# Moving hand-over, loads and the rows of maxima in the opening of a fused attention and MLP kernel

## The chip, the cores and the metric

The kernel runs as one program on one NeuronCore of a Trainium2 chip. The metric is the device time of one execution in microseconds (us), taken over three runs. A core has five engines that run their own instruction streams and meet only at semaphores: PE (matmul), DVE (vector), ACT (scalar and activation), POOL (general) and SP (which here only starts DMA transfers). On each engine, instructions start in the order in which they stand.

## The reference

One transformer block with adaptive layer norm: 2048 tokens, width 512, 32 heads of 16, an MLP with 1792 hidden units. All tensors are float32.

```python
mod = (_silu(c) @ w_mod).reshape(c.shape[0], 6, 1, -1)
sa, ca, ga, sb, cb, gb = (mod[:, 0], mod[:, 1], mod[:, 2], mod[:, 3], mod[:, 4], mod[:, 5])
h = _layernorm(x, axis=-1) * (1 + ca) + sa
x = x + ga * _A_ref(h, A_wqkv, A_wo)            # full attention, softmax over all 2048 keys
h = _layernorm(x, axis=-1) * (1 + cb) + sb
x = x + gb * _B_ref(h, B_w1, B_b1, B_w2)        # dense, Mish, dense
```

## The kernel before

**Stages.** The opening normalises x, transposes it to `h_h` (with a rounding remainder `h_l`) and makes the first keys and queries. Then come 512 steps (`t`), 16 for each of 32 groups of work. A group is four heads (two *pairs* of heads) by one block of 512 queries; a pair's keys stand in a tile `ka`, its queries in `qa` (five of each, used in turn). In one step PE makes the scores of one block of 128 keys for four heads (`score`, L637), ACT takes their exponential (L640), PE multiplies by the values `vg` (`pv`, L655), and beside this PE makes the scores of a *later* group once more, 128 queries by 512 keys at a time (L582), so that DVE can find the row maxima that softmax subtracts (L584). The remaining projections and the whole MLP are cut into small pieces and filled in between.

**Twenty steps ahead.** The maxima must be known before a group's scores can be exponentiated. So there is a lead of 20 steps, t = -20 to -1, in which no scores are used: PE makes products two at a time (`max_pair`, L596, 128 by 1024), DVE reduces them (L598), and PE fills the time with projections (L133), three or four slots after each pair of products. The lead has 40 such pairs of products: 32 for the first group (pairs 0 and 1), then 8 for the second group's first pair (pair 2, tiles `ka2` and `qa2`). Every second or third pair of products, ACT copies two numbers of the product to a tile `seen` (L601); later users of that bank of PSUM wait for the copy.

**The rows of maxima.** When the first group's 32 reductions are done, `neg_max` reduces once more (L611), PE transposes (L617), ACT and DVE make the tile `mt` (L619, L620), and four small DMAs write it into two rows of `qa0` and `qa1` (`put` in `max_rows`, L626). With these rows in place a score product comes out with its maximum already subtracted; the first is at t = 0.

**What sets the order.** Times are counted in half steps: `at(h, f)` (L206) runs f when the program is written at half step h, and step t covers h = 2t and 2t + 1. The lead is h = -40 to -1. What the change touches: `fin` of `qk_unit` (L253, brings the accumulator of a projection to SBUF as a high part and a remainder, and stores both), `slice_split` (L236, splits a slice of the weights the same way), the fills of `ka2`, `ka3`, `ka4` with ones (L562), `load_pair` (L332: two DMAs for `qa`, two for `ka`), `load_v` (L566), `early_prep` (L1585 on: splits the first MLP weights on POOL and stores them) and the `put` of L622.

**DMA issue.** All large transfers are issued by SP, in order. Every DMA signals one of eight completion semaphores, named DMAHW0 to DMAHW7 in the built program, which are handed out in turn to all DMAs, whatever engine issues them. Before a DMA is issued, its engine waits until the DMA that last had the same semaphore has landed.

Of the kernel before, what the change touches and what calls it, by code (L numbers as in the profile page):

```python
# [8 lines left out]
F32 = mybir.dt.float32  # L9
# [9 lines left out]
def adaln_block(ctx: ExitStack, tc: tile.TileContext, x, wqkv, wo, w1, b1, w2, c, w_mod, out):  # L19
    nc = tc.nc  # L20
# [8 lines left out]
    NB = S // TB  # L29
# [56 lines left out]
    def hi_copy(eng, hi, src):  # L86
        if eng == "a":
            nc.scalar.copy(hi, src)
        elif eng == "v":
            nc.vector.tensor_copy(hi, src)  # L90
        else:
            nc.gpsimd.tensor_scalar(hi, src, 1.0, 0.0, op0=ALU.mult, op1=ALU.add)

    def lo_sub(eng, lo, src, hi):
        (nc.gpsimd if eng == "p" else nc.vector).tensor_sub(lo, src, hi.bitcast(F32))  # L95
# [15 lines left out]
    def mm3(acc, ah, al, bh, bl, late="a"):  # L111

        n = len(ah)
        seq = ((ah, bh), (ah, bl), (al, bh)) if late == "a" else ((ah, bh), (al, bh), (ah, bl))
        seq = [(l[k], r[k]) for l, r in seq for k in range(n)]
        for i, (l, r) in enumerate(seq):
            mm(acc, l, r, i == 0, i == len(seq) - 1)
# [42 lines left out]
    def bank(tag="ms"):  # L160
        if not isinstance(tag, str):
            return tag
        return ring() if tag == "ring" else ps.tile([P, TB], F32, tag=tag, name="bk", bufs=1)
# [39 lines left out]
    def at(h, f):  # L203

        hooks.setdefault(h, []).append(f)
# [4 lines left out]
    ka = [kq.tile([P, S], F32R, name=f"ka{i}") for i in range(2)]  # L210
# [25 lines left out]
    def slice_split(kind, i, pool=None, eng="p", hi_eng="a"):  # L236
        raw = slices[kind, i]
        w = raw.shape[2]
        hi = (pool or qp).tile([P, DK, w], F32R, tag="wh", name="wh", bufs=2)
        lo = (pool or qp).tile([P, DK, w], F32R, tag="wl", name="wl", bufs=2)  # L240
        hi_copy(hi_eng, hi, raw)
        lo_sub(eng, lo, raw, hi)
        slices[kind, i] = (hi, lo)

    def qk_unit(kind, ct, tb, tag):

        wh, wl = slices[kind, ct]
        acc = bank(tag)
        ts_ = slice(tb * TB, (tb + 1) * TB)
        mm3(acc, [wh[:, k, :] for k in range(DK)], [wl[:, k, :] for k in range(DK)],  # L250
            [h_h[:, k, ts_] for k in range(DK)], [h_l[:, k, ts_] for k in range(DK)], "b")

        def fin(h=None):  # L253
            late = h is not None and -4 <= h < 3
            if late and not spares:
                for v in range(2):
                    both = ap.tile([P, DK, TB], F32R, tag=f"o_{v}", name="late", bufs=1)
                    spares.extend(both[:, i, :] for i in range(DK))
            if late:
                qh, ql = spares.pop(), spares.pop()  # L260
            else:
                qh = qp.tile([P, TB], F32R, tag="qh", name="qh", bufs=2)
                ql = qp.tile([P, TB], F32R, tag="ql", name="ql", bufs=2)
            if h is None:
                hi_copy("a", qh, acc)
                lo_sub("v", ql, acc, qh)
            else:
                qf = (ap.tile([P, TB], F32, tag=f"p{len(spares) // 2 % 2 * 2}", name="qf", bufs=3) if late else
                      pw.tile([P, TB], F32, tag="raw", name="qf", bufs=1))
                nc.scalar.copy(qf, acc)  # L270
                hi_copy("p", qh, qf)
                lo_sub("p", ql, qf, qh)
            scr, rows = (qscr, 50) if kind == 0 else (kscr, 48)

            def put():
                put_away.add((kind, ct, tb))
                o = 8 * ct * rows * S + tb * TB
                if kind == 0:
                    for r, src in enumerate((qh, qh, ql)):
                        nc.sync.dma_start(dap(scr, o + r * S, [[rows * S, 8], [3 * S, DH], [1, TB]]), src.bitcast(F32))  # L280
                    return
                hi = qh.bitcast(F32)
                twice = bass.AP(tensor=hi.tensor, offset=hi.offset, ap=[list(hi.ap)[0], [0, 2], [1, TB]])
                nc.sync.dma_start(dap(scr, o, [[3 * S, P], [2 * S, 2], [1, TB]]), twice)
                nc.sync.dma_start(dap(scr, o + S, [[3 * S, P], [1, TB]]), ql.bitcast(F32))

            put() if h is None else at(clear(h + (5 if h > 60 else 2)), put)
        return fin
# [48 lines left out]
    with ExitStack() as es:  # L337
# [65 lines left out]
        def apply_tb(tb):  # L403
            rs = rss.pop(tb)
            for i in range(4):
                xt = xts[4 * tb + i]
                nc.scalar.activation(xt, xt, AF.Identity, scale=rs[:, 1, i:i + 1], bias=rs[:, 2, i:i + 1])
# [115 lines left out]
        for tb in range(NB):  # L523
            if tb + 2 < NB:
                stats_tb(tb + 2)
            parts = []
            early = []
            for kind in (1, 0) if tb == 0 else (1,):
                fin = qk_unit(kind, 0, tb, "ring" if tb + 1 < NB else "ms")
                parts.append((pe_queue[2 * DK:], fin))  # L530
                early.append(pe_queue[:2 * DK])
                pe_queue.clear()
            if tb == 0:
                (kw, qw) = early
                early = [[m for k in range(DK) for m in (kw[k], qw[k], kw[DK + k])], qw[DK:]]
            pe_queue.extend(m for e in early for m in e)
            pe_run()
            if tb in (1, 2):
                for kc in (2 * tb - 2, 2 * tb - 1):
                    unit(v_unit(0, kc, "ring"))  # L540
            if tb + 1 < NB:
                tr_tb(tb + 1, CUT1)
            for late, fin in parts:
                pe_queue.extend(late)
                unit(fin)
            if tb + 1 < NB:
                tr_tb(tb + 1, CUT2)
            if tb + 2 < NB:
                apply_tb(tb + 2)
            if tb == 0:  # L550
                for pp in range(2):
                    load_q(pp, 48)
            for pp in range(2):
                if tb < 2:
                    load_k(pp, tb)
        slice_split(0, 1)


    kq2 = ctx.enter_context(tc.tile_pool(name="kq2", bufs=1))
    ka += [kq2.tile([P, S], F32R, name=f"ka{i}") for i in range(2, NR)]  # L560
    for t in ka[2:]:
        nc.gpsimd.memset(t.bitcast(F32), 1.0)  # L562
    ap = ctx.enter_context(tc.tile_pool(name="ap", bufs=1, reuse_waits="tile"))
    vgs = {}

    def load_v(n):  # L566
        assert {(2, n % G // 4, i) for i in range(NKC)} <= put_away
        t = ap.tile([P, VROW], F32, tag="vg", name="vg", bufs=2)
        nc.sync.dma_start(t, vscr[n % G])
        vgs[n] = t  # L570
# [44 lines left out]
    def max_rows(n, mm):  # L615
        pt = ring()
        nc.tensor.transpose(pt[:32, :P], mm.rearrange("p a v q -> p (a v q)"), ident)  # L617
        mh, mt = [ap.tile([32, P], F32R, tag=t, name=t, bufs=1) for t in ("mh", "mt")]
        nc.scalar.activation(mh, pt[:32, :P], AF.Identity, scale=-1.0)  # L619
        nc.vector.scalar_tensor_tensor(mt, mh.bitcast(F32), lows[:32], pt[:32, :P], op0=ALU.mult, op1=ALU.subtract)  # L620

        def put():  # L622
            for s in (1, 0):
                for j in range(2):
                    o = (2 * s + j) * 8
                    nc.sync.dma_start(  # L626
                        qa[(2 * n + j) % NR][64 * s + 48:64 * s + 50, :].rearrange("v (s q) -> v s q", s=4).bitcast(F32),
                        mt[o:o + 8, :].bitcast(F32))
        at(2 * (16 * n + 16 - PRO) + 2, put)
# [955 lines left out]
    def early_prep(i, h):  # L1585

        def split():
            scr, raw, hi, lo = raws[i]
            hi_copy("p", hi, raw)
            lo_sub("p", lo, raw, hi)  # L1590

        def put():
            scr, _, hi, lo = raws.pop(i)
            for v, part in enumerate((hi, lo)):
                nc.sync.dma_start(scr[:, v, :], part.bitcast(F32))

        at(h, split)
        at(h + 3, put)

    for i in range(EARLY):  # L1600
        early_prep(i, (-38, -36, -34, -32, -27, -25)[i])

    def start_preps(h, i=EARLY, turn=0, puts=()):

# [15 lines left out]
    for n in range(NIT):  # L1620
# [3 lines left out]
            at(32 * (n - 1), lambda n=n: load_pair(2 * n + 1))  # L1624
        if n > 0:
            at(32 * n - 11, lambda n=n: load_v(n))
    at(-7, lambda: load_v(0))
    at(17, lambda: load_pair(4))
    for qb in range(NB - 1):
        t0 = 32 * G * (qb + 1) + 16  # L1630
# [3 lines left out]
    at(2 * (T - 28), lambda: load_ys((0, 1)))  # L1634
    at(2 * (T - 12), lambda: load_ys((2,)))
    at(2 * T - 30, tail_loads)
    for pp, h in ((2, -22), (3, -10)):
        at(h, lambda pp=pp: load_pair(pp))
    def run_hooks(h):
        for f in hooks.pop(h, []):  # L1640
# [6 lines left out]
    t = T + 2  # L1647
# [32 lines left out]
```

## Time and profile before

| | before |
|---|---|
| median of three runs | 1687.12 us (1686.07 to 1687.93) |
| profiled execution | 1687.18 us |
| its span, first to last instruction | 1685.4 us |
| around the span | 1.78 us |
| PE busy in the span | 1664.2 us, 99% |
| granted PE clock | 1.00 throughout |

The profile describes the one profiled execution. "Idle before" a row is the time in which the engine had nothing to run, with the event that ended it behind the arrow; `SPq` rows are DMA issues, and the duration there is that of issuing, not of the transfer. Consecutive instructions of one kind are merged in a row (`x32`).

### The profile page before, as it was taken

How to read it: one execution, taken by the hardware profiler on the slowest of the kernel's cores; microseconds unless marked ns; L12 is line 12 of the kernel's file. 1: busy time of each engine (PE TensorE's matmuls, PEld its weight loads, DVE VectorE, ACT ScalarE, POOL GpSimd, SP SyncE). 2: the span in 40 equal slices, each digit the busy share in tenths (PEclk: the TensorE clock that was granted, in tenths of full speed). 3: DMA queues.
4: the chain of work that ended last, by engine and by line, in shares of the span. 5: the costliest groups of instructions: out<-in, count | busy, mean ns of one | idle time of the engine just before them, and what ended most of it. 6: DMA issues, size and time to landing. Idle time of an engine off the chain costs nothing.

```text
span 1685.4 us, 34363 instructions
## 1 busy us (share of the span) xinstructions
PE 1664.2 (99%) x12707; PEld 928.9 (55%) x12707; DVE 1431.5 (85%) x2372; ACT 1357.4 (81%) x2618; POOL 812.5 (48%) x839
## 2 busy tenths in 40 slices
PE   8999999999999999999999999999999999999998
PEld 6856655555445555555555455555555455555687
DVE  6988888888999988888889888888889888883377
ACT  7257777777778988888878998888878998889674
POOL 5655224755323664546323664556323664555442
PEclk9999999999999999999999999999999999999999
DMA  7886656777746334434255434534354433434261
GB/s 248 280 261 183 157 145 208 195 223 217 242 118 168 90 94 106 123 77 132 81 135 162 107 77 103 134 86 120 97 137 122 124 94 88 145 96 134 77 227 62
DMA packets 114984, 239.02 MB, mean 142 GB/s; under 512 B 24500, under 2 KB 50120, under 8 KB 108864
## 3 DMA queue, kind: packets, MB, share of 16 engines
q1 hardware_dynamic: 114808, 236.82, 49.8%
q8 instruction: 100, 1.64, 0.4%
q14 instruction: 68, 0.56, 0.1%
q10 hardware_dynamic: 8, 0.00, 0.0%
HBM read 180.48 MB, written 51.45 MB: 138 GB/s over the span
## 4 chain that ended last, share of the span: by engine, by line
PE 90%; DVE 4%; DMA 2%; ACT 2%; issue 1%; SPq 0%; POOL 0%; ACTq 0%; DVEq 0%; POOLq 0%
PE bk L655 29%; PE ring L637 22%; PE ring L582 19%; PE bk L133 12%; PE ring L1268 2%; PE ring L126 2%; DVE mx L598 1%; ACT pr L640 1%; PE bk L126 1%; DVE mx L584 1%; DMA ka<-kscr 1%; DMA wr<-in_A_wqkv 1%; DMA xt<-in_A_x 0%; PE ring L133 0%; PE ring L971 0%
## 5 line engine op out<-in xcount | busy, mean ns | idle before, releaser
L584 DVE TENSOR_REDUCE mx<-ring 128x1 f32<-128x512 f32 x1968 | 1222.4, 682 | 151.3 <-PE ring L582 134.5
L640 ACT ACTIVATE pr<-ring 128x512 f32<-128x512 f32 x2048 | 1078.2, 603 | 207.7 <-PE bk L133 112.8
L582 PE MATMUL ring<-ka,qa 64*128 64x512 f32 x1968 | 818.2, 429 | 1.4 <-ACT pr L640 1.2
L637 PE MATMUL ring<-qa,ka 64*128 64x512 f32 x2048 | 759.1, 402 | 3.3 <-ACT pr L640 1.9
L655 PE MATMUL bk<-pr,vg 128*32 128x512 f32 x4096 | 545.0, 604 | 0.0
L582 PEld LDWEIGHTS ring<-ka,qa 64*128 64x128 f32 x1968 | 350.5, 184 | 326.0 <-DVE mx L584 251.5
L637 PEld LDWEIGHTS ring<-qa,ka 64*128 64x128 f32 x2048 | 373.6, 184 | 191.4 <-DVE mx L584 113.3
L133 PE MATMUL bk<-h,w 64*128 64x512 f32 (+1 forms) x1080 | 278.0, 390 | 0.0
L133 PE MATMUL bk<-w,a_h 64*128 64x512 f32 x632 | 210.8, 413 | 0.0
L133 PEld LDWEIGHTS bk<-h,w 64*128 64x128 f32 x1080 | 178.4, 184 | 8.9 <-ACT pr L640 1.5
L655 PEld LDWEIGHTS bk<-pr,vg 128*32 128x32 f32 x4096 | 81.1, 108 | 135.8 <-issue 126.5
L133 PE MATMUL bk<-w,a_l 64*128 64x512 f32 x316 | 124.0, 393 | 0.0
L133 PEld LDWEIGHTS bk<-w,a_h 64*128 64x128 f32 x632 | 106.7, 184 | 3.2 <-ACT hb L849 0.8
L1027 POOL TENSOR_TENSOR y<-yd,y 128x512 f32<-128x512 f32 x44 | 56.8, 1292 | 88.9 <-ACT yd L1026 79.5
L861 POOL TENSOR_SCALAR qq<-ee 128x512 f32<-128x512 f32 x25 | 15.5, 621 | 169.4 <-ACT ee L855 169.4
L877 POOL TENSOR_TENSOR qq<-qq,rr 128x512 f32<-128x512 f32 x42 | 54.1, 1289 | 86.0 <-ACT rr L871 86.0
L863 POOL TENSOR_TENSOR hb<-hb,ee 128x512 f32<-128x512 f32 x42 | 54.1, 1289 | 79.7 <-DVE ee L859 77.7
L133 PE MATMUL bk<-w,o_hl 64*128 64x512 f32 x288 | 79.3, 405 | 0.0
L95 POOL TENSOR_TENSOR a_l<-hb,a_h 128x512 fp32r<-128x512 f32 x53 | 73.0, 1378 | 4.4
L133 PE MATMUL bk<-h_h,wl 64*128 64x512 f32 x192 | 62.0, 416 | 0.3 <-ACT pr L640 0.3
L133 PEld LDWEIGHTS bk<-w,a_l 64*128 64x128 f32 x316 | 58.3, 184 | 2.8
L879 POOL TENSOR_TENSOR rr<-rr,qq 128x512 f32<-128x512 f32 x42 | 54.1, 1289 | 3.5
(234 smaller groups left out, 1889.6 us busy)
## 6 DMA issues: line engine op xcount, KB each, us to landing
ka<-kscr SPq DMA_DIRECT2D x124, 384.0 KB
w<-w2scr SPq DMA_DIRECT2D x56, 512.0 KB
w<-w1scr SPq DMA_DIRECT2D x46, 512.0 KB
vg<-vscr SPq DMA_DIRECT2D x32, 552.0 KB
qa<-qscr SPq DMA_DIRECT2D x124, 100.0 KB
qscr<-qh SPq DMA_DIRECT2D x32, 256.0 KB
w2scr<-hl SPq DMA_DIRECT2D x14, 512.0 KB
kscr<-qh SPq DMA_DIRECT2D x12, 512.0 KB
```

The source lines that it names most:

```text
L95: (nc.gpsimd if eng == "p" else nc.vector).tensor_sub(lo, src, hi.bitcast(F32))
L126: nc.tensor.matmul(acc, l, r, start=start, stop=stop)
L133: i = nc.tensor.matmul(acc, l[64 * g:64 * g + 64], r[64 * g:64 * g + 64], start=start and not then, stop=bool(stop and then))
L582: nc.tensor.matmul(pm, qt[64 * s:64 * s + 64, qs * P:(qs + 1) * P], kt[64 * s:64 * s + 64, kb * TB:(kb + 1) * TB], start=True, stop=True)
L584: nc.vector.tensor_reduce(out=mxs[n][:, s, 4 * j + qs, kb:kb + 1], in_=pm, op=ALU.max, axis=AX.X)
L637: nc.tensor.matmul(p_, kt[64 * s:64 * s + 64, kc * P:(kc + 1) * P], qt[64 * s:64 * s + 64, :], start=True, stop=True)
L640: e = nc.scalar.activation(pr, p_, AF.Exp, scale=SCALE)
L655: nc.tensor.matmul(accs[n][32 * h:32 * h + 32, :], vgs[n][:, o:o + 32], pts.pop((t, h)), start=(kc == 0), stop=(kc == 15))
L863: (nc.vector if tail else nc.gpsimd).tensor_mul(hb, hb, ee)
L877: nc.gpsimd.tensor_mul(qq, qq, rr)
L879: nc.gpsimd.tensor_mul(rr, rr, qq)
L1027: nc.gpsimd.tensor_add(y[i], yd, y[i])
```

## The change

Five places move; the computation stays the same.

```diff
@@ qk_unit / fin
-            if h is None:
+            if h is None and (kind, tb) != (1, NB - 1):
                 hi_copy("a", qh, acc)
                 lo_sub("v", ql, acc, qh)
             else:
@@ opening, loop over tb
             if tb + 2 < NB:
                 apply_tb(tb + 2)
+            elif tb + 1 < NB:
+                slice_split(0, 1)
...
-        slice_split(0, 1)
-
...
-    for t in ka[2:]:
-        nc.gpsimd.memset(t.bitcast(F32), 1.0)
+    for i, h in ((2, -39), (3, -39), (4, -18)):
+        at(h, lambda t=ka[i]: nc.gpsimd.memset(t.bitcast(F32), 1.0))
@@ max_rows / put
-                    nc.sync.dma_start(
+                    (nc.scalar if n == 0 else nc.sync).dma_start(
@@ schedule
-        early_prep(i, (-38, -36, -34, -32, -27, -25)[i])
+        early_prep(i, (-38, -36, -34, -27, -25, -23)[i])
...
-    at(-7, lambda: load_v(0))
+    at(-3, lambda: load_v(0))
...
-    for pp, h in ((2, -22), (3, -10)):
+    for pp, h in ((2, -36), (3, -2)):
         at(h, lambda pp=pp: load_pair(pp))
```

The last keys of the opening go through ACT and POOL (copy to `qf`, then high part and remainder on POOL) instead of ACT and DVE. The split of the second query slice is done one round of the opening loop sooner. The fills of `ka2` and `ka3` move one half step into the lead, that of `ka4` to h = -18. Pair 2 is loaded at h = -36 instead of -22, pair 3 at -2 instead of -10, the first values at -3 instead of -7. Three of the six early weight preparations come later. The four DMAs of the first group's rows of maxima are issued by ACT; those of all later groups stay on SP.

On SP, at the end of the lead, this stood before (`vscr` is the store of the values, `vq` the tile they come from; the bracket names the semaphores that the row waits for):

```order
L306 DMA vscr_67<-vq_115 128x4x272 [waits DMAHW7_49,Activation_49]
L306 DMA vscr_67<-vq_113 128x4x272 [waits DMAHW0_49,Activation_49]
L321 DMA qa3_103<-qscr_66 50x512 [waits DMAHW1_49]
L321 DMA qa3_103<-qscr_66 50x512 [waits DMAHW2_49]
L330 DMA ka3_694<-kscr_65 48x2048 [waits DMAHW3_49]
L330 DMA ka3_694<-kscr_65 48x2048 [waits DMAHW4_49]
L284 DMA kscr_65<-qh_1232 128x2x512 [waits DMAHW5_49,Pool_49]
L285 DMA kscr_65<-ql_1233 128x512 [waits DMAHW6_49,Pool_49]
L569 DMA vg_1296<-vscr_67 128x1104 [waits DMAHW7_49,DMAHW0_49]
L626 DMA qa0_100<-mt_1315 2x4x128 [waits DVE_49,PE_49]
L626 DMA qa1_101<-mt_1315 2x4x128 [waits DMAHW1_49,PE_49]
```

And now:

```order
L306 DMA vscr_67<-vq_115 128x4x272 [waits DMAHW7_49,Activation_49]
L306 DMA vscr_67<-vq_113 128x4x272 [waits DMAHW0_49,Activation_49]
L284 DMA kscr_65<-qh_1234 128x2x512 [waits DMAHW1_49,Pool_49]
L285 DMA kscr_65<-ql_1235 128x512 [waits DMAHW2_49,Pool_49]
L233 DMA wr_1342<-in_A_wqkv 128x4x128 [waits DMAHW3_49]
L569 DMA vg_1347<-vscr_67 128x1104 [waits DMAHW7_49,DMAHW4_49,DMAHW0_49]
L321 DMA qa3_103<-qscr_66 50x512 [waits DMAHW5_49]
L321 DMA qa3_103<-qscr_66 50x512 [waits DMAHW6_49]
L330 DMA ka3_696<-kscr_65 48x2048 x2
```

Pair 2 has gone up ahead of all the weight stores, pair 3 has moved behind the load of the values, and the rows of maxima have left this queue. The first store of keys takes DMAHW1, the second DMAHW2, the values DMAHW4 and the first load of `qa3` DMAHW5.

On ACT, at the same place, this stood before (`mh` is the first half of the rows of maxima, `seen` the copy of L601, `qf` a projection on its way to SBUF):

```order
L270 COPY qf_1234<-bk_1052 128x512 [waits Activation_49,Pool_49]
L601 COPY seen_1281<-ring_94 128x2 [waits DVE_49,Activation_49]
L619 ACTIVATE mh_1314<-ring_94 32x128 [waits PE_49]
L601 COPY seen_1336<-ring_94 128x2 [waits DVE_49,Activation_49]
L270 COPY qf_1372<-ring_94 128x512 [waits PE_49]
L270 COPY qf_1376<-ring_94 128x512 [waits PE_49]
```

And now:

```order
L601 COPY seen_1279<-ring_94 128x2 [waits DVE_49,Activation_49]
L619 ACTIVATE mh_1310<-ring_94 32x128 [waits PE_49]
L626 DMA qa0_100<-mt_1311 2x4x128 [waits DMAHW1_49,DVE_49]
L626 DMA qa1_101<-mt_1311 2x4x128 [waits DMAHW2_49]
L626 DMA qa0_100<-mt_1311 2x4x128 [waits DMAHW4_49]
L626 DMA qa1_101<-mt_1311 2x4x128 [waits DMAHW5_49]
L601 COPY seen_1332<-ring_94 128x2 [waits DVE_49,Activation_49]
L270 COPY qf_1374<-ring_94 128x512 [waits PE_49]
```

The four DMAs stand between `mh` and the last `seen` of the lead, and each waits for one of the semaphores just named. In the built program the counts that they wait for are reached only when the two stores of keys, the load of the values and the first load of `qa3` have landed.

On PE the order has not changed. Of the eight pairs of products of pair 2, two stand ahead of the transpose L617 and six behind it. The fourth of those six (called F below, since the eight are A to H) waits for ACT: it takes the bank of PSUM that the last `seen` copy of the lead reads, and in the built program the count it waits for is that of this copy.

## The prediction

> **What bounds the kernel now.** I read the page's busy shares first, then the windows, then the timeline of each engine up to t = 0.
>
> ```profile
> PE 1664.2 (99%) x12707; PEld 928.9 (55%) x12707; DVE 1431.5 (85%) x2372; ACT 1357.4 (81%) x2618; POOL 812.5 (48%) x839
> 0.00:98.00 98.00, 86.92 (x794) 72.85 (x796) 79.76 (x113) 42.31 (x74) 52.70 (x82) 1.00 0.85 268
> 98.00:200.00 102.00, 101.39 (x911) 59.74 (x908) 88.25 (x148) 79.79 (x163) 51.23 (x44) 1.00 0.66 188
> 200.00:1685.00 1485.00, 1475.91 (x11011) 796.32 (x11007) 1263.44 (x2112) 1235.33 (x2382) 708.53 (x714) 1.00 0.47 130
> ```
>
> The second and third numbers of a window row are its length and PE's busy time. From 98 us on PE is busy 99.4% of the time, so whatever moves the start of t = 0 moves the end by the same amount, up or down. No part of the diff takes work from PE. The change can only act before t = 0, where PE has 98.00 - 86.92 = 11.08 us of idle time. That part is bound by DVE:
>
> ```profile
> 46.90 0.49 PE L596 MATMUL ring<-ka,qa 64*128 64x512 f32 x2
> 47.67 0.69 DVE L95 TENSOR_TENSOR ql<-bk,qh 128x512 fp32r<-128x512 f32 x1 [1.26 <-ACT qh L88]
> 48.28 36.34 DVE L598 TENSOR_REDUCE mx<-ring 128x2 f32<-128x1024 f32 x32
> 84.65 0.34 DVE L611 TENSOR_REDUCE mm<-mx 128x16 f32<-128x64 f32 x2
> 87.50 2.36 DVE L598 TENSOR_REDUCE mx<-ring 128x2 f32<-128x1024 f32 x2 [2.50 <-PE ring L596]
> 89.77 0.33 DVE L620 SCALAR_TENSOR_TENSOR mt<-mh,lows,ring 32x128 fp32r<-32x128 f32 x1
> 90.45 7.02 DVE L598 TENSOR_REDUCE mx<-ring 128x2 f32<-128x1024 f32 x6 [0.35 <-PE ring L596]
> 97.52 0.50 PE L637 MATMUL ring<-qa,ka 64*128 64x512 f32 x1 [0.43 <-DVE mx L598]
> ```
>
> The reader should see one chain: 32 reductions back to back, a gap of 2.50 us, two reductions of pair 2 (A and B), the rows of maxima, six more (C to H), t = 0. The gap comes from PE, and PE waits for the load of pair 2:
>
> ```profile
> 86.04 0.46 PE L596 MATMUL ring<-ka,qa 64*128 64x512 f32 x1 [2.40 <-DMA ka<-kscr]
> 86.99 0.47 PE L596 MATMUL ring<-ka,qa 64*128 64x512 f32 x1 [0.48 <-DMA ka<-kscr]
> ```
>
> The profiled execution took 1687.18 us, its span 1685.4, so 1.78 lies around it; the median of the three runs is 1687.12, 0.06 below. I sum against the profiled one.
>
> **The hand-over.** The first pair of products starts at 46.90 and takes 0.49; DVE could reduce it some 0.05 later, at 47.44. It starts at 48.28, since DVE first waits 1.26 for ACT's `qh` and then spends 0.69 on `ql`. Both leave DVE: gain 48.28 - 47.44 = 0.84 us. POOL takes them over:
>
> ```profile
> 49.46 5.30 POOL L562 MEMSET ka<- 128x2048 f32 x3
> 67.86 0.62 POOL L92 TENSOR_SCALAR qh<-qf 128x512 fp32r<-128x512 f32 x1
> 68.56 1.29 POOL L95 TENSOR_TENSOR ql<-qf,qh 128x512 fp32r<-128x512 f32 x1
> 79.35 1.29 POOL L95 TENSOR_TENSOR wl<-wr,wh 128x512 fp32r<-128x512 f32 x1 [5.57 <-ACT wh L88]
> ```
>
> That is 0.62 + 1.29 = 1.91 us more for POOL, against one fill of 5.30 / 3 = 1.77 that leaves this place for h = -18, where POOL sits idle for 5.57. The two fills left end near 53, nine us before SP now reaches the loads of pair 2. Were that cover gone, the fills would delay the loads by what they are late. The earlier `slice_split(0, 1)` spares PE a wait, but DVE is the bound there: nothing.
>
> **Pair 2 at -36, the preparations.** SP would issue the four loads near 62, ahead of the weight stores, instead of at 77.44, and they need nothing later than the keys of the opening:
>
> ```profile
> 62.22 5.54 SPq L1595 DMA_DIRECT2D w1scr<-ep  x8
> 68.00 0.63 SPq L233 DMA_DIRECT2D wr<-in_A_wqkv  x1
> 77.44 1.59 SPq L321 DMA_DIRECT2D qa<-qscr  x2
> 79.12 0.77 SPq L330 DMA_DIRECT2D ka<-kscr  x2
> 79.99 0.93 SPq L306 DMA_DIRECT2D vscr<-vq  x2
> ```
>
> They then land before 84.99 (84.65 + 0.34), when DVE wants A: the whole 2.50 goes. Everything put behind them is later by their bytes, the slice `wr` among it (1 to 3 us, my estimate); ACT needs that slice near 77 and F, below, waits longer. The later preparations meet POOL's idle time: nothing. With nothing else changed, t = 0 would come 0.84 + 2.51 = 3.35 us sooner (2.51 is 87.50 - 84.99), at 94.17, and the run take 1683.8. Pair 3 is first used in t = 4 and the values in t = 2, at 104.57 below:
>
> ```profile
> 104.57 1.06 PE L655 MATMUL bk<-pr,vg 128*32 128x512 f32 x8
> 108.48 0.72 PE L582 MATMUL ring<-ka,qa 64*128 64x512 f32 x2
> ```
>
> **The four DMAs on ACT.** This is the term that turns the sign. A DMA's issue waits for the landing of the DMA that last had its semaphore, and the engine stands there. The trace shows such waits on SP, where data give no reason for them (a store of keys waiting for a load of another tile, a store waiting for the values):
>
> ```profile
> SPq L284 <- DMA ka<-kscr: 1.5, 1, 1.5
> SPq L284 <- DMA vg<-vscr: 1.1, 1, 1.1
> SPq L569 <- DMA vscr<-vq: 2.8, 2, 1.5
> 90.16 0.33 SPq L569 DMA_DIRECT2D vg<-vscr  x1
> 90.59 3.02 SPq L626 DMA_DIRECT2D qa<-mt  x4
> 97.71 0.37 SPq L284 DMA_DIRECT2D kscr<-late  x1
> ```
>
> On SP such a wait cost little, because only transfers stood behind it. On ACT the order now has, behind `mh`: `mt` 1 (waits for the store of key high parts), `mt` 2 (the store of remainders), `mt` 3 (the load of the values, `vg`), `mt` 4 (the first load of `qa3`), then the last `seen`. PE's F waits for that `seen`, and everything on PE stands behind F.
>
> ```profile
> 92.92 0.16 ACT L601 COPY seen<-ring 128x2 f32<-128x2 f32 x1 [3.32 <-DVE mx L598]
> 93.48 0.39 PE L596 MATMUL ring<-ka,qa 64*128 64x512 f32 x2
> 73.39 0.16 ACT L601 COPY seen<-ring 128x2 f32<-128x2 f32 x1 [3.23 <-DVE mx L598]
> 73.61 0.50 PE L596 MATMUL ring<-ka,qa 64*128 64x512 f32 x2 [0.16 <-ACT seen L601]
> ```
>
> When does `vg` land? It is issued once the last stores of values (`vscr`) have landed, at 90.16. Pair 2 and the weight stores are put ahead of those stores in both orders, only their sequence differs, so I leave 90.16. Its transfer is not paired with a landing in the trace, so I bound it by three rows: 3.60 us for an input load on the chain of waits, below; 68.00 - 62.22 = 5.78 between the first weight store and the `wr` that waits for it, with eight weight stores in the queue; and 97.71 - 90.16 = 7.55 between `vg` and the store that waits for it, when pair 3 was still ahead of it in the queue.
>
> ```profile
> 19.27 3.60 DMA xt<-in_A_x
> L626 SPq DMA_DIRECT2D qa<-mt x4: 613/632/711, 90.6 to 93.0; - x4
> ```
>
> Now the two stores of keys and one `wr` are in front of `vg`, and pair 3 is behind: I take 5.78, the row whose backlog is nearest. So `vg` lands at 95.94, and ACT has two issues left at 0.63 (the middle number of the row): free at 97.20. `seen` takes 0.16, F follows 0.06 after it (73.39 + 0.16 to 73.61): F at 97.42. From F to t = 0 it is 97.52 - 93.48 = 4.04, DVE's three reductions with it: t = 0 at 101.46. That is 3.94 later than before, after the 3.35 have been gained and lost again. Predicted: 1687.18 + 3.94 = **1691.1**. With the ends 3.60 and 7.55: 1688.9 and 1692.9, the range of this case alone. If `vg` went out 1 us earlier or later, so would the end. What decides is when ACT comes free: before 93.26 the change is a gain (93.48 - 0.22), and at 89.9 (90.13 - 0.22, with 90.13 = 93.48 - 3.35) the full 3.35 is kept.
>
> The rows written by `mt` 1 and 2, which t = 0 reads, need no more than the stores of keys; they go out well before 97 and don't decide.
>
> A rule of the Trainium skill speaks to both sides of this. "DMA: Bandwidth & Descriptors", section "Anatomy of one DMA — SWDGE (gpsimd) path", says that DMA engines do not wait on semaphores, any wait takes place on the issuing sequencer; though written for another path, it agrees with the SP rows above and would put the stall on ACT as summed. The section "Queues, rings and completion order" says that each DMA engine goes round the queues that hold work, packet by packet; by that, rows on a queue of ACT's own would pass SP's backlog, which is what the first rival says. No run here shows that yet.
>
> **The rivals.**
>
> ```profile
> ka<-kscr SPq DMA_DIRECT2D x4, 384.0 KB
> qa<-qscr SPq DMA_DIRECT2D x4, 100.0 KB
> SPq L1595 <- POOL ep L95: 2.9, 3, 1.5
> ```
>
> *The other side: a hold that does not last.* If the stores, `vg` and the first `qa3` land by 88.6 (two issues before 89.9), ACT is never late, the small rows pass the backlog, and the gain stands: 1683.8. For it: with pair 3 out of the way (two loads of 384 KB and two of 100 KB, 0.99 MB), less stands in the queue in front of `vg`; at the lead's 268 GB/s that is 3.7 us of traffic. Against it: `vg` cannot be issued before the `vscr` stores land, and pair 3 stood behind those stores, not in front; 90.16 would have to become 83. Chance 0.12.
>
> *The hold eats just the gain.* Stores in front of the `vscr` stores drain sooner because POOL delivers the preparations later, `vg` goes out near 88 and takes 3.6 to 5: ACT free between 92.9 and 94.3, and the run ends between 1686.8 and 1688.2, by the same sum; with half a microsecond of spread on each side, 1686 to 1689. For it: SP waits 2.9 us for POOL's pieces in this stretch, which could be put to use. Against it: DMA is busy 85% on average and nothing carries fewer bytes. Chance 0.17.
>
> *A longer hold.* Pair 2 taken early pushes every later transfer; the last `vscr` lands 1.5 us later, and `vg` takes 7.55 as before. Then ACT is free at 100.5 and the run takes 1687.18 + 3.94 + 1.5 + 1.77 = 1694.4. For it: the queue is full from 60 to 98. Against it: the same transfers were ahead of `vscr` before. Chance 0.07.
>
> *The change doesn't do what it says.* The rows of maxima are "issued by ScalarE", but t = 0 may not start sooner for it: it waits for DVE's last reduction by 0.43, not for `mt`. That is so in all the cases above, and part of the forecast.
>
> **How the numbers follow.** A measurement of this kernel can tell about 0.2%, 3.4 us: below 1683.75 is faster, above 1690.5 slower. The forecast has 0.64, of which its range of 1688.9 to 1692.9 lies mostly above that bound: 0.48 slower, 0.16 same. The longer hold adds 0.07 slower, the balanced case 0.17 same. The first rival, at the very bound, I count as faster, 0.12. In sum: 0.12 faster, 0.33 same, 0.55 slower. The range of 1686.0 to 1693.0 holds the forecast and the balanced case and leaves out the two outer ones, 0.19.
>
> **What would show it.** In the timeline after, DVE's first reduction near 47.4 (hand-over right) and A's reduction at once behind L611, without the 2.50 (pair 2 right). On ACT four issues behind `mh`, with a long idle time ended by the landing of `vg`, the last `seen` near 97.2 and F near 97.4: the hold. PE's wait for `seen` in front of F should be near 7 us (97.42 - 90.13). What would prove the forecast wrong: `seen` before 93.3; `vg` issued well before 90; a PE wait for `mt`, `vg` or pair 3 after t = 0; or idle time of PE after 98 us larger than before.

## The result: slower by 0.31%, and where the time stands

| | before | changed |
|---|---|---|
| median of six runs | 1686.57 us | 1692.01 us |
| ratio to before, 95% interval | | 1.0031 [1.0021, 1.0041] |
| profiled execution, its span | 1687.18 us, 1685.4 | 1694.30 us, 1692.5 |
| first product of the lead (L596) to t = 0, profiled | 50.62 us | 55.24 us |

The last row (46.90 to 97.52 before, 46.87 to 102.11 after) is the measure I use below: the start of the lead itself wanders by up to 1.7 us between executions of these kernels (45.81 to 47.47), and this difference does not contain it. All ratios are to the kernel before, run beside each version on the same chip. One execution of experiment 9, of 2561.74 us at a mean granted clock of 0.556, is left out of its ratio. The profiled execution of the change is the slowest of its six.

First the timeline of DVE after the change, in the lead:

```profile
47.44 36.30 DVE L598 TENSOR_REDUCE mx<-ring 128x2 f32<-128x1024 f32 x32 [1.05 <-PE ring L596]
83.77 0.34 DVE L611 TENSOR_REDUCE mm<-mx 128x16 f32<-128x64 f32 x2
84.03 2.35 DVE L598 TENSOR_REDUCE mx<-ring 128x2 f32<-128x1024 f32 x2
86.29 0.33 DVE L620 SCALAR_TENSOR_TENSOR mt<-mh,lows,ring 32x128 fp32r<-32x128 f32 x1
86.97 3.52 DVE L598 TENSOR_REDUCE mx<-ring 128x2 f32<-128x1024 f32 x3 [0.36 <-PE ring L596]
96.67 1.23 DVE L598 TENSOR_REDUCE mx<-ring 128x2 f32<-128x1024 f32 x1 [6.17 <-PE ring L596]
```

The reader should see both gains and the loss. The first reduction starts 0.57 us after the first product (it was 1.38), A and B follow L611 at once (2.50 us were in between), and after the third of the six others there is a hole of 6.17 us that before did not have. Now ACT's timeline at that hole, with its DMA issues (ACTq):

```profile
85.62 0.27 ACT L619 ACTIVATE mh<-ring 32x128 fp32r<-32x128 f32 x1 [1.64 <-PE ring L617]
88.27 7.17 ACTq L626 DMA_DIRECT2D qa<-mt  x4
95.55 0.16 ACT L601 COPY seen<-ring 128x2 f32<-128x2 f32 x1 [9.66 <-DMA qa<-qscr]
```

and PE's:

```profile
95.76 0.80 PE L596 MATMUL ring<-ka,qa 64*128 64x512 f32 x2 [5.60 <-ACT seen L601]
...
102.11 0.50 PE L637 MATMUL ring<-qa,ka 64*128 64x512 f32 x1 [0.38 <-DVE mx L598]
```

Four issues of 0.62 to 0.75 us each took 7.17 us in all, `seen` came 9.66 us after `mh`, and F (the first row of PE's) waited 5.60 us for `seen`. The piece of the chain of waits (start, duration, what) says which landing it was:

```profile
80.29 6.65 DMA vscr<-vq
...
86.95 0.33 SPq L569
...
87.33 7.47 DMA qa<-qscr
...
94.82 0.62 ACTq L626
...
95.55 0.16 ACT seen L601
```

The store of values lands, SP issues `vg` (L569) and the first load of `qa3` behind it, that load lands at 94.80, and ACT can issue the fourth row of maxima. This is the hold of the prediction, one row of the program after another. The windows show something that the prediction did not have (the PE clock is the first number after the five engines' busy times):

```profile
90.00:92.00 2.00, 0.16 (x2) 0.00 (x0) 0.50 (x1) 0.00 (x0) 0.00 (x0) 1.00 1.20 296
92.00:94.00 2.00, 0.00 (x0) 0.00 (x0) 0.00 (x0) 0.00 (x0) 0.00 (x0) 0.95 0.90 183
94.00:96.00 2.00, 0.24 (x2) 0.24 (x4) 0.00 (x0) 0.45 (x2) 0.00 (x0) 0.50 0.97 137
96.00:98.00 2.00, 2.00 (x10) 1.59 (x12) 1.23 (x1) 0.69 (x2) 1.63 (x2) 0.50 1.02 243
98.00:100.00 2.00, 2.00 (x12) 1.56 (x10) 1.23 (x1) 0.00 (x0) 1.92 (x3) 0.50 1.06 358
100.00:102.00 2.00, 1.73 (x12) 1.01 (x10) 1.17 (x1) 0.20 (x1) 0.23 (x1) 0.84 1.06 404
```

PE stands idle, its clock goes to half at 93.8, and when PE goes on at 95.76 it stays half until 100.6 (0.5 for 6.8 us in all, by these rows). F to t = 0 takes 6.35 us (95.76 to 102.11); it was 4.04.

### The profile page after: what moved, and what is told of

It is laid out like the page before. It is cut to its first block, busy times and chain, and to the rows that moved or that the text cites. A ratio compares the mean times of both kernels' runs of the same rounds, so it can differ in the third digit from the quotient of the medians.

```text
span 1692.5 us, 34362 instructions
## 1 busy us (share of the span) xinstructions
PE 1669.1 (99%) x12707; PEld 932.3 (55%) x12707; DVE 1431.7 (85%) x2371; ACT 1357.6 (80%) x2618; POOL 814.9 (48%) x841
## 4 chain that ended last, share of the span: by engine, by line
PE 89%; DVE 4%; DMA 3%; ACT 2%; issue 1%; SPq 1%; POOL 0%; ACTq 0%; DVEq 0%; POOLq 0%
PE bk L655 29%; PE ring L637 22%; PE ring L582 19%; PE bk L133 12%; PE ring L1268 2%; PE ring L126 2%; DVE mx L598 1%; ACT pr L640 1%; DVE mx L584 1%; PE bk L126 1%; DMA ka<-kscr 1%; DMA qa<-qscr 0%; PE ring L971 0%; DMA qa<-mt 0%; PE ring L133 0%
```

## The experiments

**1. Only the issuing engine put back.**

```diff
-                    (nc.scalar if n == 0 else nc.sync).dma_start(
+                    nc.sync.dma_start(
```

> The change with one part undone: the four DMAs of the rows of maxima are issued by SP again. In the built program their issues then wait only for weight stores that left long before. Theory of the hold (ACT waits for transfers, F waits for ACT): no idle time before F, F near 90.1 and t = 0 near 94.2, the granted PE clock 1.00 around it, and the run 3.3 us below before (1683.3 if before is 1686.6). Rival (the early pair 2 and the late pair 3 and values cost the time, whoever issues the rows): t = 0 is early, but PE waits for keys or values in the first steps, and the run is at least 1688.

Measured: 0.9977 [0.9969, 0.9986], and 0.9978 [0.9970, 0.9987] when the same kernel ran again (experiment 10); the first product to t = 0 takes 47.18 and 47.17 us, 3.44 less than before. ACT in the timeline:

```profile
85.94 0.27 ACT L619 ACTIVATE mh<-ring 32x128 fp32r<-32x128 f32 x1 [1.64 <-PE ring L617]
89.76 0.16 ACT L601 COPY seen<-ring 128x2 f32<-128x2 f32 x1 [3.55 <-DVE mx L598]
```

and SP's issues:

```profile
87.00 2.78 SPq L626 DMA_DIRECT2D qa<-mt  x4
...
90.26 0.50 SPq L569 DMA_DIRECT2D vg<-vscr  x1
```

`seen` now waits for DVE as it did before, and the rows leave SP in 2.78 us, ahead of `vg`. So the rest of the change is a gain, and all that the change lost hangs on the issuing engine. The rival that blamed the moved loads falls.

**2. Only the issuing engine changed, all else as before.**

```diff
-                    nc.sync.dma_start(
+                    (nc.scalar if n == 0 else nc.sync).dma_start(
```

> Before, with one part of the change: only the four DMAs on ACT. Their issues now wait for a store of values, a load of qa3, a load of ka3 and the last store of key high parts. Theory of the hold: that store landed near 95.5 in before (SP's second load of wm waited for it until 95.53), so ACT is free near 96.1 and F starts near 96.4 in place of 93.48: t = 0 2.9 us later, 4 if the PE clock drops in the gap; the run at 1689.5 to 1690.6 if before is 1686.6. Rival (a DMA issued by ACT costs only its issue of 0.63 us, four of them hidden before F): within 0.5 us of before.

Measured: 1.0025 [1.0016, 1.0034], 4 us. Its chain of waits:

```profile
85.94 9.79 DMA kscr<-qh
...
95.75 0.62 ACTq L626
...
96.48 0.17 ACT seen L601
```

and F in PE's timeline:

```profile
96.69 0.50 PE L596 MATMUL ring<-ka,qa 64*128 64x512 f32 x2 [2.14 <-ACT seen L601]
```

The store that the built program names, landing at 95.73, and F at 96.69: 0.3 us from the expected times. t = 0 came 4.87 later than before, at 102.39, which is more than expected: F is 3.21 later, and F to t = 0 took 5.70 in place of 4.04, with the clock at half for 3.4 us of it. (The clock was also at half after the gap ahead of A, see the last section; PE still waited 2.14 us for ACT after that, so it did not set F.) What ACT pays is not the issue of 0.62 us but the wait until another transfer, picked by its turn at the semaphores, has landed.

**3. Other transfers in the same turn.**

```diff
-    at(-3, lambda: load_v(0))
+    at(0, lambda: load_v(0))
-    for pp, h in ((2, -36), (3, -2)):
+    for pp, h in ((2, -36), (3, 1)):
```

> The change, with the loads of the values and of pair 3 put three half steps later still, so that the rows of maxima, still on ACT, take semaphores whose last users are the two last stores of values and the two stores of keys. Theory of the hold: ACT is free when the store of key remainders has landed, near 90.1 by the second issue after the change: F near 91, t = 0 near 95.1, 2.4 us below before (1684.2 if before is 1686.6), unless pair 3, now behind four more stores, is late for t = 4. Rival (the ACT queue itself is the cost): F and t = 0 as after the change, near 95.8 and 102.1, and at least 1691.

Measured: 0.9989 [0.9980, 0.9998], 2 us below before; the first product to t = 0 takes 47.85. ACT's timeline:

```profile
86.93 3.60 ACTq L626 DMA_DIRECT2D qa<-mt  x4
90.63 0.16 ACT L601 COPY seen<-ring 128x2 f32<-128x2 f32 x1 [4.46 <-DMA qa<-mt]
```

and PE's F:

```profile
90.84 0.50 PE L596 MATMUL ring<-ka,qa 64*128 64x512 f32 x2 [0.40 <-ACT seen L601]
```

The rows are on ACT as in the change, and the hold is 0.40 us in place of 5.60, since in the built program older transfers had the same semaphores. F and t = 0 (at 95.00) came where the theory had them, and PE waits for no key in the first steps. The later loads also take traffic out of this stretch, so this experiment alone would not separate the two; experiments 1, 2 and 7, in which only the issuing engine changes, do.

**4. Products in the gap.**

```diff
+                if t == -2 and i:
+                    for _ in range(22):
+                        nc.tensor.matmul(ring_t[:, (ring_at[0] - 2) % ring_of[0], :], h_h[:, 0, :P], h_h[:, 0, :TB],
+                                         start=True, stop=True)
                 max_pair(tm // 16, jq, kb)
```

> The change, with 22 more matmuls (128 by 512, result not used) on PE right ahead of F, in the bank of E, some 5 us of work: they fill the gap in which PE waits for ACT. Theory that the idle gap itself halves the PE clock afterwards: F still near 95.8, but the granted clock stays at 1.00, F to t = 0 takes 4.0 and not 6.35, t = 0 near 99.8 and the run 2.3 us below the change (1689.7 if the change is at 1692.0). Rival (the clock falls for another reason in this stretch, as load of memory): the clock is 0.50 after F all the same and the run is at 1692 or more.

Measured: 1.0011 [1.0002, 1.0020], beside 1.0031 and 1.0029 for the change. With more work on PE the kernel is some 3 us faster. PE's timeline (L1407 are the added products):

```profile
89.61 5.28 PE L1407 MATMUL ring<-h_h 128*128 128x512 f32 x22 [0.39 <-DVE mx L598]
95.00 0.50 PE L596 MATMUL ring<-ka,qa 64*128 64x512 f32 x2
...
99.16 0.49 PE L637 MATMUL ring<-qa,ka 64*128 64x512 f32 x1 [0.43 <-DVE mx L598]
```

and the window from 96 us:

```profile
96.00:98.00 2.00, 2.00 (x20) 1.63 (x18) 2.00 (x3) 0.00 (x0) 1.92 (x3) 1.00 1.10 256
```

F is held to 95.00 all the same, the clock stays at 1.00, and F to t = 0 takes 4.16. Between the profiled executions of this kernel and of experiment 8, 1.8 us lie in the lead (53.23 from the first product to t = 0, against 55.00) and 2.4 after t = 0 (1587.2 to the last instruction, against 1589.7), where waits wander (see below). The mean granted clock of the ten executions here is 0.999 or 1.000, that of the fifteen of the change 0.996 to 0.998, so the one trace is no exception. In this stretch the idle time is what halves the clock; the load of memory, as high here, does not.

**5. The hand-over alone,** from before.

```diff
-            if h is None:
+            if h is None and (kind, tb) != (1, NB - 1):
...
+            elif tb + 1 < NB:
+                slice_split(0, 1)
...
-        slice_split(0, 1)
```

> Before, with the hand-over and the earlier split of the second query slice alone; pair 2, pair 3, values, preparations, fills and the rows of maxima as before. Theory: the first reduction starts near 47.4, 0.84 us sooner, but A still waits for the load of pair 2, which lands when it did (86.0): DVE's gap before A grows from 2.50 to 3.3 and t = 0 stays at 97.5, the run within 0.5 us of before, or some 2 us more if the longer gap lowers the PE clock. Rival (the hand-over is worth its 0.84 by itself, as a term of a sum): t = 0 at 96.7, 0.84 us below before.

Measured: 0.9998 [0.9989, 1.0007]. The interval does not tell the two theories apart, and the trace does so only in part. DVE and, behind it, PE in the timeline, and a window:

```profile
46.65 36.30 DVE L598 TENSOR_REDUCE mx<-ring 128x2 f32<-128x1024 f32 x32 [1.05 <-PE ring L596]
```

```profile
84.74 0.76 PE L596 MATMUL ring<-ka,qa 64*128 64x512 f32 x1 [2.76 <-DMA ka<-kscr]
```

```profile
84.00:86.00 2.00, 1.09 (x3) 0.64 (x5) 0.00 (x0) 0.00 (x0) 0.00 (x0) 0.50 1.09 348
```

The first reduction comes 0.57 us after the first product (46.08), so the 0.81 are won there; A then waits 2.76 for pair 2 instead of 2.40, and in this execution the clock also went to half in the gap: 51.69 from the first product to t = 0, 1.07 more than before. The load landed 1.3 us sooner than in before (84.7 and 86.0), in a lead that began 0.8 sooner, and that was not foreseen. So at full clock some 0.5 us of the 0.8 could have been left (1.3 - 0.8, an estimate from these rows); that A waits for pair 2 is shown, that the hand-over alone is worth nothing is not.

**6. Pair 2 early, without the hand-over,** from the kernel of experiment 1.

```diff
-            if h is None and (kind, tb) != (1, NB - 1):
+            if h is None:
...
-            elif tb + 1 < NB:
-                slice_split(0, 1)
...
+        slice_split(0, 1)
```

> The change without the hand-over and the earlier split, and with the rows of maxima on SP. Theory: the 2.50 us before A are gone, nothing else: first reduction near 48.3, A right behind L611 near 85.0, t = 0 at 95.0 and the run 2.5 us below before, 0.84 above the kernel that has both. Rival (pair 2 early only brings another transfer late): a PE wait for a load in the lead or in the first steps, and less than 1 us of gain.

Measured: 0.9982 [0.9973, 0.9990]; first product to t = 0 48.05 us, 2.57 less than before and 0.87 more than with both. So the hand-over is worth its 0.8 us once pair 2 is early, and before that no gain can be seen (5). The two kernels' intervals overlap, and the 0.87 is a reading of the traces.

**7. The rows issued by POOL.**

```diff
-                    (nc.scalar if n == 0 else nc.sync).dma_start(
+                    (nc.gpsimd if n == 0 else nc.sync).dma_start(
```

> The change, with the four DMAs of the first group's rows of maxima issued by POOL in place of ACT. In the built program they take none of the eight semaphores and wait for DVE and PE alone; POOL has nothing between 81 and 94 us. Theory of the hold: no wait before F, t = 0 near 94.3, the run 3.3 us below before, as with the rows on SP. Rival (small DMAs from an engine of their own are late behind the full queue): t = 0 waits for the rows of maxima, 1685 or more.

Measured: 0.9984 [0.9974, 0.9993], 47.18 us from the first product to t = 0. The four issues, in POOL's timeline, take 2.44 us and wait for no transfer:

```profile
88.00 2.44 POOL L626 DMA_DIRECT2D qa<-mt  x4 [5.68 <-PE ring L596]
```

t = 0 waits for DVE's last reduction, as in before, and not for the rows. So the eight semaphores are not handed out to all DMAs whatever engine issues them, as the part on DMA issue has it: here those of SP and ACT take them, those of POOL do not.

**8. The change again.**

> The changed kernel itself, beside the runs of this call, to compare with the kernel with products in the gap and to see the spread of its times. Expected: F held to 95 to 97, t = 0 at 101 to 103, 1690 to 1694; whether the wait of 1.5 us for a pair of keys near 417 us is there again is open.

Measured: 1.0029 [1.0019, 1.0038], 1689.23 to 1693.79 us. F held to 95.23, t = 0 at 101.14, 55.00 us after the first product. The wait at 417 us was not there; one of 1.82 us, for rows of maxima, stood at 381.

**9. The early gains with the loads of before,** from the kernel of experiment 1.

```diff
-    at(-3, lambda: load_v(0))
+    at(-7, lambda: load_v(0))
-    for pp, h in ((2, -36), (3, -2)):
+    for pp, h in ((2, -36), (3, -10)):
```

> The hand-over and pair 2 early, as in the change, with the rows of maxima on SP and the loads of pair 3 (h = -10) and of the values (-7) where before had them. On SP the rows then stand behind the load of the values, and behind loads of qa3 and ka3 whose semaphores they take. Theory (the later loads serve to let the rows go out early): the rows are issued from 90 to 93.5 in place of 87 to 89.8, t = 0 or t = 1 waits for them, 0.5 to 2 us worse than with the later loads (1684 to 1685.5, where the kernel with the later loads has 1683.5). Rival (the later loads are worth nothing, the rows land in time either way): equal within 0.3 us.

Measured: 0.9997 [0.9988, 1.0005]: the whole gain is gone, more than expected. SP's issues, PE's timeline, and the window after it:

```profile
89.69 3.15 SPq L626 DMA_DIRECT2D qa<-mt  x4
```

```profile
91.37 0.41 PE L596 MATMUL ring<-ka,qa 64*128 64x512 f32 x2
...
95.94 0.76 PE L637 MATMUL ring<-qa,ka 64*128 64x512 f32 x1 [3.26 <-DMA qa<-mt]
```

```profile
96.00:98.00 2.00, 2.00 (x10) 1.73 (x12) 1.22 (x2) 1.00 (x2) 1.70 (x2) 0.50 0.95 286
```

The lead's last product is done at 91.8, but the rows, issued from 89.69 behind `vg`, arrive at 95.9; PE waits 3.26 us and goes on at half clock. The later loads of values and pair 3 are thus what lets the rows out in time when SP issues them.

**10. Experiment 1 again,** on the chip of experiment 9: its numbers stand at experiment 1.

> The change with the rows of maxima on SP, once more, beside the kernel with the old loads on the same chip. Expected: t = 0 near 94.3, no wait before F, 3.3 us below before.

The version of experiments 1 and 10 beats both kernels: 3.7 us below before by the ratio, 9 below the change.

## Why the prediction was right, step by step

It forecast 1691.1, 3.9 us above before, and slower; 1692.01 was measured, 5.2 above before by the ratio. Its mechanism is shown, by experiments 1, 2, 3 and 7. That the number came so close is partly luck. In the profiled execution F came 1.66 us sooner than summed, F to t = 0 took 2.31 more, and the stretch from t = 0 to the end 2.53 more. That execution, the slowest of its six, ended at 1694.30, 3.2 above the forecast and outside its range; the median lies inside.

- **The hand-over, 0.84, and pair 2, 2.51.** Measured 0.87 (experiments 1 and 6) and 2.57 (6 and before), 3.44 in all against 3.35. The sum held; as terms they are not independent, since A waits for pair 2 as long as that is late (5).
- **"Pair 2 and the weight stores are put ahead of those stores in both orders, ... so I leave 90.16."** Off by 3.2 us: `vg` left at 86.95. In the second execution of the change it was 89.01, so a part of this wanders. But the same set ahead does not mean the same landing. From the end of the issue of the last two stores of values to that of `vg` it took 9.2 us before (80.92 to 90.16) and 6.0 in both executions of the change (80.96 to 86.95, 82.98 to 89.01). Pair 3, which in before went out right behind these stores, does not explain it: in experiment 9 it did so again, and the time was 6.3 (83.00 to 89.27). In experiments 2 and 5, where pair 2 kept its old place right ahead of the stores, it was 8.5 and 9.0. So the longer time goes with the place of pair 2, the sequence that the prediction took to make no difference; whether that alone makes it was not tried.
- **The landing, 5.78.** `vg` is issued at 86.95, and ACT's third issue, which waits for it, goes out at 93.63, 6.7 us later and not 5.78. The first load of `qa3`, which the sum had counted as landed by then, lands later still, at 94.80: 7.85 us after `vg` was issued, above even the upper end I had taken (7.55). So one issue of 0.62 was left to ACT, not two. With these sizes F came at 95.76, not 97.42. In the second execution (8) the path was the one of the sum: ACT's third issue at 93.64, 4.6 us after `vg`, the fourth right behind it, F at 95.23.
- **F to t = 0, 4.04 "with DVE's three reductions".** This took the clock as given. It was 6.35 after the long idle time, 4.16 when the gap was filled (4). The 1.7 us that F came sooner went here, and 0.65 more.
- **"From 98 us on ... whatever moves the start of t = 0 moves the end by the same amount".** Not to the last microsecond. In the profiled execution t = 0 is 4.59 later and the end 7.12. From t = 0 to the end PE is idle for 10.92 us in place of 10.09, and busy for 1.68 more with the same work. A wait for rows of maxima has gone from 0.59 us (at 376 us) to 0.36 (at 380), and a new one for keys stands at 417. PE's timeline of before, then of the change, then two windows of the change:

```profile
376.30 0.47 PE L637 MATMUL ring<-qa,ka 64*128 64x512 f32 x1 [0.59 <-DMA qa<-mt]
```

```profile
417.04 0.47 PE L582 MATMUL ring<-ka,qa 64*128 64x512 f32 x1 [1.50 <-DMA ka<-kscr]
```

```profile
418.00:420.00 2.00, 2.00 (x15) 0.60 (x12) 1.44 (x3) 1.47 (x3) 1.83 (x3) 0.52 0.58 147
420.00:422.00 2.00, 2.00 (x15) 0.76 (x9) 0.34 (x2) 0.27 (x1) 1.92 (x3) 0.63 0.82 246
```

The clock is at half for 1.92 and 1.48 us of these windows, 3.4 us that do the work of 1.7, which is the 1.68 of more busy time. In the other execution of the change it was a wait of 1.82 for rows at 381 us, with a halved clock too. Every trace has one such wait for rows, of 0.2 to 1.9 us, be t = 0 late or early (0.36 in the change, 1.42 in experiment 7); what sets its length is open.
- **What was costed at nothing.** The fills, the preparations and the later `wr` cost nothing that shows: the 3.44 leave no room for it. The later loads of the values and of pair 3 were given no worth at all, only slack. With the rows on SP they carry the gain (9); with the rows on ACT they put `vg` and `qa3` into the turns that the rows then waited for (3).
- **The rivals.** The first, that the hold does not last, would need the landings by 88.6; the first two rows were issued from 88.27 on and the last at 94.82. The second, that the hold eats just the gain, would need ACT free by 94.3; it was at 95.44. One of its conditions, that `vg` goes out near 88, came true; the short landing did not. The third, a longer hold, had the stores of values land later; they landed sooner. Two of the signs named against the forecast came true: `vg` left well before 90, and PE's idle time behind t = 0 grew, by 0.83 us. They changed sizes; F still waited for `seen`. No run has the rows on ACT's queue behind no wait at all with SP's backlog beside them, so whether a second queue is served sooner stays open. The stall on the issuing engine is what the Trainium skill says of DMAs that GpSimd issues ("DMA: Bandwidth & Descriptors", section "Anatomy of one DMA — SWDGE (gpsimd) path"), and here it is the ACTq rows that show it.

## What to carry to other kernels

A DMA moved to a compute engine brings its waits along: in a program that hands out completion semaphores in turn, look up which transfer had the same semaphore last and when it lands, and what stands behind the DMA on its new engine. A wait that costs nothing in front of other DMAs can cost 5 us in front of a copy of 0.16 us. And a gap on PE can cost twice, once by its length and once by the clock after it: here 5.60 us, and then 2.2 between F and t = 0 (6.35 against 4.16).

## What the runs showed of the hardware

**The PE clock after a gap.** It goes to 0.50 for 3.4 us or for twice that (6.8 after the change's gap of 5.60, and after one of 2.76 in experiment 5). This begins, or goes on, when PE is busy again; 3.4 us of PE's work at half clock cost 1.7 us. It is not certain for a given gap. Experiment 2 and before have a gap in the same place, ahead of A. Windows of experiment 2, whose gap was 2.04 us:

```profile
85.00:86.00 1.00, 0.00 (x0) 0.01 (x1) 0.30 (x2) 0.16 (x1) 0.00 (x0) 1.00 1.01 345
86.00:87.00 1.00, 0.50 (x3) 0.24 (x3) 0.00 (x0) 0.00 (x0) 0.00 (x0) 0.93 1.12 361
87.00:88.00 1.00, 1.00 (x6) 0.87 (x8) 0.24 (x1) 0.00 (x0) 0.00 (x0) 0.50 1.16 374
...
90.00:91.00 1.00, 0.96 (x6) 0.28 (x5) 0.76 (x1) 0.19 (x1) 0.00 (x0) 0.86 0.89 174
```

and one of before, whose gap was 2.40:

```profile
87.00:88.00 1.00, 1.00 (x9) 0.96 (x11) 0.50 (x1) 0.00 (x0) 0.00 (x0) 1.00 1.16 370
```

In the one the clock is halved from 86.9 to 90.3, in the other it stays at 1.00. With a gap of 1.50 us at 417, in the change, it fell, with one of 1.42 in experiment 7 (at 374) it did not.

The Trainium skill has this in "TensorE: Matmul & The Clock Gate", section "Part 1: The HAM clock gate (the "warmup" mystery)": half clock after an idle window of about 3.4 us, and full clock after a busy one, where the windows run freely. The length and the chance agree with these traces; that a whole idle window is needed does not, since gaps of 2.04 and 1.50 us were enough here.
